# A fused attention and two-mixture kernel: rounding of h, one weight factor, router rounds and x sums issued at other products of the second mixture

## The chip, the cores and the metric

The kernel runs on one core of one Trainium2 chip. The metric is the device time of one execution in microseconds (us). Five engines work side by side, each through its own list of instructions in order: TensorE (PE, with PEld for its weight loads), VectorE (DVE), ScalarE (ACT), GpSimd (POOL) and SyncE (SP, which here only issues transfers). They wait for each other through semaphores.

## The reference

Three stages follow each other. Each step below computes only the third.

```python
# 1. clustered attention, 2 x 8 heads, 768 positions, 64 wide -> x (1536 tokens x 512)
# 2. first mixture: h = x @ w_in (512 x 2048); x = silu(h) @ w_out
# 3. second mixture: 8 experts, 1024 wide each
logits = x @ w_gate
P = np.exp(logits - logits.max())
for _ in range(8):                       # the router: 8 rounds
    P /= P.sum(1, keepdims=True) + 1e-09
    P /= P.sum(0, keepdims=True) + 1e-09
    P *= N / E
for e in range(E):
    h = np.maximum(x @ w1[e], 0.0)
    out += P[:, e:e + 1] * (h @ w2[e])
```

## The kernel before

**The stage in question.** The second mixture runs in 16 steps (`s` from 0 to 15), each half an expert: 512 of its 1024 hidden columns. A step is 14 turns of a loop over `n` (`s, i = divmod(n, 14)`, L1325). Turns 0 to 6 compute h = x @ w1, turns 7 to 13 compute h @ w2. Each of the two is a block product with 7 multiplications in place of 8 (Strassen's scheme), so most turns hold one *product*: 7 sums of blocks are multiplied and added into four results. One of the seven in the first layer is done once more in the same way on quarter blocks (`quad`, L1016: seven small products into the banks `q` and, in turn 7, `r`).

**Two parts for each factor.** TensorE multiplies fp32r. Each factor is split into a rounded part and a rest, and three matmuls (`hi*hi`, `hi*lo`, `lo*hi`) stand for one (L645). The rounded part of a weight factor is `wfh`, a copy by ScalarE (`factor_hi`, L848); the rest `wfl` is a subtraction by VectorE (`factor_lo`, L842). For h the parts are `ah` (`h_hi`, L1067, ScalarE) and `al` (`h_lo`, L1077, VectorE), each in two halves k = 0 and 1, of 768 tokens each. In the program's full names `ah3_9_1` is the rounded second half of the factor for scheme number 3 in step 9. There are four buffers for `ah` and four for `al`.

**Order.** The engines follow the order in which Python issues the instructions (`manual_schedule`, L1323): in each turn first the evacuation of the product before, then the preparation of factors for later products, then the matmuls of the turn's own product. Products of the second layer are multiplied half by half: 18 matmuls of 256 columns that use half 0 of h, then 18 that use half 1.

**Evacuation.** The second layer's scheme numbers come in the order 1, 5, 6, 3, 7, 2, 4 (turns 7 to 13). Numbers 1, 6, 7, 4 add up in one set of three PSUM banks and 5, 3 in another, and after each product the set is scaled by the router's column `Pg` and copied into a staging slot (`evacuate_b`, L1106; `acc` in the trace). So the set that a product adds into must have been evacuated during the product before it. In turns 11 and 12 VectorE copies the last bank, otherwise ScalarE copies all three (six instructions). A transfer of 768 KB then adds the slot to the output, issued by GpSimd (L1146). Slots are four slices of the buffer `acc1`, taken in turn (`stage`, L1101). In step 0 two of these slices still hold x.

**First layer.** `evacuate_a` (L1148) adds or copies the banks into h: by ScalarE (`copy_out`, `L1061`) or VectorE (`add_out`, the adds at L747). In turn 5 VectorE adds product 4 into the block `22`; ScalarE copies the same banks into the block `21` as soon as each add has read and written, then applies Relu to `22` in place (L1163). In turn 6 VectorE adds product 5 into `12`. Turn 6 has no product of its own in steps 1 to 15; turn 7 mixes the quarter products `r` with the first product of the second layer (L1041). `h_s1` to `h_s4` form the block sums of h on VectorE (L1165 to L1182).

**Router.** A generator `gate` (L940) holds the router; each `next(gating)` at the end of a turn issues it up to the next `yield`. A round is nine small VectorE instructions with one 8-column matmul `col` between them (L982 to L995).

**x sums.** `x4_sums` (L898) forms four sums of quarters of x in place in slice 3 of `acc1` on VectorE; `x4_rest(i)` (L903) splits one of them into its two parts (one ScalarE copy, one VectorE subtraction, 128x384). The quarter products `r` use them from step 1 on.

Of the kernel before, what the change touches and what calls it, by code (L numbers as in the profile page):

```python
# [38 lines left out]
def attention_moe_kernel(ctx, tc, kq, vp, cent, w_in, w_out, w_gate, w1, w2, out):  # L39
# [406 lines left out]
    with tc.manual_schedule(engines={ENG.PE, ENG.DVE, ENG.Activation, ENG.Pool, ENG.SP}):  # L446
# [147 lines left out]
        for pair in range(-4, NPAIR + 4):  # L594
            for item in ORDER:
                kind, at, *place = item.split(",")
                f, stride, low, high = KINDS[kind]
                i = int(at) + stride * pair
# [304 lines left out]
    def x4_rest(*which):  # L903
        hi, lo = (t[:, 3:] for t in x4)
        for i in which:
            act.copy(hi[:, i], x4_sum(i))
            lo_of(vec, lo[:, i], x4_sum(i), hi[:, i])
# [187 lines left out]
        return to[i * HT : (i + 1) * HT, j * HD : (j + 1) * HD].rearrange("(t p) d -> p t d", p=P)  # L1095

    stages, stores = [0], [0]
    RING = (0, 1, 2, 0, 1, 2, 0)
    kept = {}

    def stage():  # L1101
        stages[0] += 1
        n = stages[0] - 1
        return acc2[:, RING[n] if n < 7 else (3, 1, 2, 0)[(n - 7) % 4]]

    def evacuate_b(n, by_vec=0):  # L1106

# [86 lines left out]
    for s in range(NS1):  # L1194
        n = 2 * s + 1
# [122 lines left out]
    Pg = sk.tile([P, TT, E], F32, name="Pg")  # L1318

    gating = None  # L1320
    acc2 = acc1.rearrange("p k (t d) -> p k t d", d=HD)
    ENG = mybir.EngineType
    with tc.manual_schedule(engines={ENG.PE, ENG.DVE, ENG.Activation, ENG.Pool}):  # L1323
        psn = {}
        for n in range(14 * NS + 1):  # L1325
            s, i = divmod(n, 14)

            if i == 8:
                h_hi(s, 6, 1)
            if i == 2 or i == 7 and s:  # L1330
                pass
            elif n and i <= 7 and i > 0:
# [20 lines left out]
            if i == 1:  # L1353
                quad_add(s, 1)
                quad_add(s, 2)
                if s == 0:
                    x_factor(5, (0, 1))
                else:
                    quad_sums(s, True)
                if s == 1:  # L1360
                    x4_rest(0, 1)
            if i == 3:
                factor(n + 2, vec)
                factor(n + 3, vec)
# [7 lines left out]
                factor(n + 3, vec)  # L1372
                w_t3(n + 3, vec)
            if i == 4 + (s == 0):
                h_hi(s, 1, 0, relu=True)
                h_hi(s, 1, 1, relu=True)
                h_lo(s, 1, 0, relu=True)
                h_lo(s, 1, 1, relu=True)
            if i in (5, 6, 7) and 3 <= s < 7:
                for m in (2 * i - 10, 2 * i - 9):  # L1380
                    gps.tensor_scalar(out=again[:, m], in0=again[:, m], scalar1=Pg[:, 6 * block[0] + m, 0:1], scalar2=1.0, op0=ALU.mult, op1=ALU.mult)
                if i == 7:
                    gps.dma_start(out=out_block(*block), in_=again, accum_op=ALU.add)
            if i == 5 or i == 6 and s == 0:
                factor(n + 3, vec)
            if i == 5 and s == 0:
                x4_sums()
            if i == 6:
                h_s1(s, (0,))
                h_hi(s, 5, 0)  # L1390
# [10 lines left out]
                kept[1, 0] = stage()  # L1401
                nc.sync.dma_start(out=kept[1, 0], in_=out_block(1, 0))
            if i == 8:
                h_lo(s, 6, 1)
                h_s3(s)
            lates = {8: 3, 9: 7, 10: 2, 11: 4}
            late = lates.get(i - 1)
            if late:
                h_hi(s, late, 1, late == 2)
                h_lo(s, late, 1, late == 2)  # L1410
            if i == 9:
                h_s4(s)
            late = lates.get(i)
            if late:
                h_hi(s, late, 0, late == 2)
                h_lo(s, late, 0, late == 2)
            if i in (8, 9):
                factor(n + 2, vec)
            if i in (10, 11, 12, 13):
                if i == 11:  # L1420
                    w_t4(n - 4, vec)
                if i == 12:
                    w_load(n + 9)
                    w_sums1(n + 2, vec)
                factor(n + 2, vec)
                if i == 13:
                    quad_sums(s + 1)
            p = order(n)[i % 7]
            if i == 0:
                g = groups1(n, ready.pop(n), xf[1])  # L1430
                sets[n // 7, 1] = [ps3.tile([P, 512], F32, name=f"a{s}_1_{u}", tag="s") for u in range(3)]
                psn[n] = psn[n + 2] = sets[n // 7, 1]
                multiply(psn[n], g[:2], True)
                quad(s, 1)
                multiply(psn[n], g[2:], True)
                quad(s, 2)
            elif i == 1:
                g = groups1(n + 1, ready.pop(n + 1), xf[6])
                quad(s, 5)
                multiply(psn[n + 1], g[:1], False)  # L1440
                quad(s, 6)
                multiply(psn[n + 1], g[1:2], False)
                quad_add(s, 5)
                quad_add(s, 6)
                if s == 0:
                    x_sum((0, 0), t2, (0, 0), (0,))
            elif i == 2:
                quad(s, 7)
                multiply(psn[n], g[2:3], False)
                quad(s, 3)  # L1450
                multiply(psn[n], g[3:], False)
                quad_add(s, 7)
                if s == 0:
                    x_sum((0, 0), t2, (0, 0), (1,))
                quad(s, 4)
                quad_add(s, 3)
                if s == 0:
                    x_factor(7, (0, 0), (0,))
                quad_add(s, 4)
                ready.pop(n - 1)  # L1460
                factor(n + 2, vec)
                if s == 0:
                    x_factor(7, (0, 0), (1,))
                    x_factor(3, (1, 1))
                w_sums1(n + 5, vec)
                if s == 1:
                    x4_rest(2, 3)
            elif i == 6:
                if s == 0:
                    psn[n] = whole4(s, n)  # L1470
            elif i < 7:
                psn[n] = product(n, groups1(n, ready.pop(n), xf[p]))
            elif i == 7 and s:
                for q in (2, 1, 5):
                    quad(s, q, True)
                g = groups2([hf.pop((s, p, k)) for k in range(2)], ready.pop(n))
                psn[n] = sets[n // 7, 1] = [ps3.tile([P, 512], F32, name=f"b{s}_1_{u}", tag="s") for u in range(3)]
                opened = set()
                half_product(psn[n], g, 0, slice(0, 6), opened)
                quad_add(s, 2, True)  # L1480
                quad_add(s, 1, True)
                quad_add(s, 5, True)
                h_s1(s, (1,))
                h_hi(s, 5, 1)
                quad(s, 6, True)
                quad(s, 3, True)
                half_product(psn[n], g, 1, slice(0, 3), opened)
                quad_add(s, 6, True)
                h_lo(s, 5, 0)
                factor(n + 2, vec)  # L1490
                quad_add(s, 3, True)
                quad(s, 7, True)
                half_product(psn[n], g, 1, slice(3, 6), opened)
                quad_add(s, 7, True)
                h_lo(s, 5, 1)
                quad(s, 4, True)
                ready.pop(n - 1)
                h_s2(s, (0,))
                h_hi(s, 6, 0)
                quad_add(s, 4, True)  # L1500
                h_s2(s, (1,))
                h_lo(s, 6, 0)
            else:
                psn[n] = product(n, groups2([hf.pop((s, p, k)) for k in range(2)], ready.pop(n)), by_half=n < 14 * NS - 1)
# [3 lines left out]
            if gating is not None:  # L1508
                if s == 2 and i == 7:
                    for _ in gating:  # L1510
                        pass
                elif s == 0 or s < 3 and 2 <= i < 7 - s % 2 or s == 1 and i > 9:
                    next(gating, None)


# [36 lines left out]
```

## Time and profile before

| what | us |
| --- | --- |
| median of 3 runs | 1522.07 |
| lowest, highest | 1521.46, 1524.11 |
| the profiled execution's own time | 1523.46 |
| its span in the trace | 1521.7 |

The trace is of one execution. Its rows name an engine, a line, an operation and `out<-in` by the program's names without buffer numbers. Idle time that stands in brackets at a row is the time just before it in which its engine did nothing, and what ended it. A matmul's duration in the trace is longer than the distance to the next one, since matmuls overlap; how far TensorE is behind is read from the distances of their starts. The attention and the first mixture take the first 486 us, and the second mixture the rest.

### The profile page before, as it was taken

Reading aid. Unit: us, or ns where it says so; the run is one execution under the profiler, and the core shown is the slowest. Engines: PE = TensorE matmul, PEld = TensorE weight load, DVE = VectorE, ACT = ScalarE, POOL = GpSimd, SP = SyncE. Lnnn points to the kernel's source line nnn. Section 1 sums busy time; section 2 is a strip of 40 time slices with the busy share of each in tenths; the row PEclk is TensorE's granted clock in tenths of the full one; section 3 lists DMA queues with packets and bytes.
Section 4 is the critical chain, followed back from the end, with each engine's and each line's share of the span. In section 5 each row is a group of like instructions: output and inputs, shape, how many; then the busy total and the mean of one; then the engine's idle time right before and its main releaser. Section 6 shows DMA issues by size and latency. Waiting matters only on the chain.

```text
span 1521.7 us, 25357 instructions
## 1 busy us (share of the span) xinstructions
PE 1460.9 (96%) x9703; PEld 1298.5 (85%) x9704; DVE 1207.8 (79%) x2045; ACT 965.4 (63%) x1848; POOL 367.4 (24%) x356
## 2 busy tenths in 40 slices
PE   8999999999999999989999999999999999999997
PEld 5777778888888888889989889898898988999887
DVE  7788888678888878877887778778777777877777
ACT  7776777564563574656757667576675766757654
POOL 6776741212110010102212232021120211201111
PEclk9999999999999999999999999999999999999998
DMA  7667501212120072928769697494784947849566
GB/s 223 169 160 197 145 29 56 70 56 83 56 84 1 29 173 48 161 83 180 114 129 185 109 192 116 87 180 78 143 131 80 190 67 138 137 84 182 81 114 125
DMA packets 136314, 177.49 MB, mean 117 GB/s; under 512 B 6272, under 2 KB 108672, under 8 KB 136192
## 3 DMA queue, kind: packets, MB, share of 16 engines
q0 software_dynamic: 83584, 87.30, 38.0%
q1 hardware_dynamic: 51104, 87.32, 19.1%
q8 instruction: 76, 1.25, 0.3%
q10 hardware_dynamic: 1504, 1.25, 0.2%
q14 instruction: 46, 0.38, 0.1%
HBM read 65.36 MB, written 88.87 MB: 101 GB/s over the span
## 4 chain that ended last, share of the span: by engine, by line
PE 41%; DVE 19%; ACT 18%; issue 6%; ACTq 0%; DVEq 0%
PE b L652 12%; PE a L652 11%; PE y L706 9%; DVE h L747 6%; ACT acc L1137 6%; PE q L1021 4%; ACT ah L1074 3%; PE l L652 3%; ACT wfh L863 2%; DVE wfl L750 2%; DVE al L1082 2%; ACT h L1061 2%; DVE h L1168 2%; ACT h L1163 2%; DVE al L750 1%
## 5 line engine op out<-in xcount | busy, mean ns | idle before, releaser
L652 PE MATMUL b<-wfh,ah 128*128 128x256 f32 x1164 | 335.5, 288 | 14.1 <-ACT acc L1137 6.5
L652 PE MATMUL b<-wfh,al 128*128 128x256 f32 x1164 | 332.5, 286 | 4.6 <-DVE al L750 4.6
L652 PE MATMUL b<-wfl,ah 128*128 128x256 f32 x1164 | 331.7, 285 | 0.0
L1146 POOL DMA_DIRECT2D out_dram<-acc x87 | 126.2, 1580 | 618.6 <-ACT acc L1137 480.1
L1074 ACT CAST ah<-h 128x768 fp32r<-128x768 f32 x160 | 136.5, 853 | 181.0 <-DVE h L1168 83.1
L652 PEld LDWEIGHTS b<-wfh,ah 128*128 128x128 f32 x1164 | 223.4, 192 | 21.3 <-ACT acc L1137 9.4
L652 PEld LDWEIGHTS b<-wfh,al 128*128 128x128 f32 x1164 | 223.6, 192 | 8.2 <-DVE al L750 7.7
L652 PEld LDWEIGHTS b<-wfl,ah 128*128 128x128 f32 x1164 | 223.7, 192 | 2.2 <-DVE wfl L750 0.9
L652 PE MATMUL a<-xfh,wfh 128*128 128x512 f32 (+1 forms) x640 | 216.1, 338 | 0.4 <-ACT h L1061 0.2
L652 PE MATMUL a<-xfl,wfh 128*128 128x512 f32 (+1 forms) x640 | 215.8, 337 | 0.0
L652 PE MATMUL a<-xfh,wfl 128*128 128x512 f32 (+1 forms) x640 | 215.5, 337 | 0.0
L750 DVE TENSOR_TENSOR al<-h,ah 128x768 fp32r<-128x768 f32 x160 | 152.8, 955 | 77.8 <-ACT ah L1074 74.0
L1137 ACT ACTIVATE acc<-b,Pg 128x256 f32<-128x256 f32 x512 | 199.4, 507 | 0.0
L1061 ACT COPY h<-a 128x512 f32<-128x512 f32 x192 | 111.9, 605 | 136.2 <-PE a L652 92.2
L652 PEld LDWEIGHTS a<-xfh,wfh 128*128 128x128 f32 x640 | 121.1, 189 | 12.8 <-ACT h L1061 1.3
L652 PEld LDWEIGHTS a<-xfh,wfl 128*128 128x128 f32 x640 | 120.9, 189 | 12.9
L652 PEld LDWEIGHTS a<-xfl,wfh 128*128 128x128 f32 x640 | 121.1, 189 | 10.4
L313 ACT ACTIVATE p<-s,m 128x768 f32<-128x768 f32 x96 | 86.7, 905 | 39.4 <-DVE m L304 36.9
L304 DVE TENSOR_REDUCE m<-s 128x1 f32<-128x768 f32 x96 | 90.0, 951 | 13.5 <-PE s L297 13.1
L323 POOL TENSOR_SCALAR p<-p,rec 128x768 f32<-128x768 f32 x96 | 86.7, 915 | 48.6 <-DVE rec L318 41.4
L750 DVE TENSOR_TENSOR wfl<-w1r,wfh 128x512 fp32r<-128x512 f32 x80 | 55.0, 688 | 53.1 <-ACT wfh L863 53.1
L747 DVE TENSOR_TENSOR h<-q,h 128x384 f32<-128x384 f32 x112 | 60.8, 554 | 36.8 <-PE q L1021 34.8
(260 smaller groups left out, 3404.3 us busy)
## 6 DMA issues: line engine op xcount, KB each, us to landing
out_dram<-acc POOLq DMA_DIRECT2D x91, 768.0 KB, 9.3
w0r<-in_w_dram SPq DMA_DIRECT2D x16, 1024.0 KB, 5.1
w1r<-in_w_dram SPq DMA_DIRECT2D x16, 1024.0 KB, 6.6
qk<-qk SPq DMA_DIRECT2D x45, 192.0 KB, 3.5
wr<-in_w_in_dram SPq DMA_DIRECT2D x16, 512.0 KB, 3.7
wr<-in_w_out_dram SPq DMA_DIRECT2D x16, 512.0 KB, 3.5
first_out<-acc POOLq DMA_DIRECT2D x10, 768.0 KB, 10.5
raw<-in_kq_dram SPq DMA_DIRECT2D x16, 384.0 KB, 4.4
```

The costliest lines, as they stand in the source:

```text
L304: nc.vector.tensor_reduce(out=m, in_=tiles[i]["s"][:, :S], axis=AX.X, op=ALU.max, negate=True)
L313: nc.scalar.activation(t["p"], t.pop("s")[:, :S], AF.Exp, bias=t.pop("m"), accum_out=chunks[c]["sum"][:, j, 0:1])
L323: nc.gpsimd.tensor_scalar(out=p, in0=p, scalar1=chunks[c]["rec"][:, j : j + 1], scalar2=1.0, op0=ALU.mult, op1=ALU.mult)
L652: nc.tensor.matmul(ps[u][:, cols], lhsT=lf(i, k), rhs=rt(j, k), start=fresh and u not in opened, stop=k == 1 and q == 2, skip_group_check= ...
L706: nc.tensor.matmul(out, lhsT=w[:, k, d * P : (d + 1) * P], rhs=g, start=first, stop=last, skip_group_check=True)
L747: e.tensor_tensor(out=out, in0=in0, in1=in1, op=op)
L750: e.tensor_tensor(out=lo, in0=x, in1=r(hi), op=ALU.subtract)
L1021: nc.tensor.matmul(ps, lhsT=quad_lhs(s, q, a, four), rhs=(x4 if four else xq)[b][:, XQ[q]], start=j == 0 and q in (1, 2, 5), stop=j == 2, ...
L1061: act.copy(bank(t, u), ps[u])
L1074: act.copy(hi, x)
L1137: act.mul(t[:, 2 * u + m], z[:, m], g)
L1146: gps.dma_start(out=to, in_=t, accum_op=ALU.add)
```

## The change

It touches only the loop over `n` of the second mixture. No instruction's work changes; on TensorE only a few of the router's `col` matmuls stand elsewhere.

- **Second halves of h.** In turns 8 to 12 the second half of the factor for the next product (`h_hi(s, late, 1)`, and its `h_lo`) is issued at the head of the turn, ahead of the evacuation. Before, it came after the evacuation (for number 6, only its `h_lo` did).
- **One weight factor.** In turn 5 `factor_hi(n + 3)` (the rounded part of the weight factor for product 8) is issued ahead of `evacuate_a`, and its `factor_lo` after it. Before, both came after. In step 0 the Relu casts of number 1 move ahead of it too.
- **x sums.** `x4_sums` moves from turn 5 of step 0 to turn 11; `x4_rest(0)` and `(1)` from turn 1 of step 1 to turns 12 and 13 of step 0, `x4_rest(2)` and `(3)` from turn 2 of step 1 to places between the quarter adds of its turns 1 and 2.
- **Slots.** Since slice 2 holds x for longer, the ring of slots of the first two steps is written down anew: in step 0 slices 0 and 1 alternate, slice 2 comes fifth.
- **Router rounds.** Steps 1 and 2 draw `next(gating)` in turns 2, 3 (twice) and 4, where it was turns 2 to 5 (step 1) and 2 to 6 (step 2). Step 0 and turns 10 to 13 of step 1 draw as before.

```diff
-    RING = (0, 1, 2, 0, 1, 2, 0)
+    RING = (0, 1, 0, 1, 2, 0, 1)
...
-        return acc2[:, RING[n] if n < 7 else (3, 1, 2, 0)[(n - 7) % 4]]
+        return acc2[:, RING[n] if n < 7 else (3, 0, 2, 1)[(n - 7) % 4]]
...
+    LATES = {7: 6, 8: 3, 9: 7, 10: 2, 11: 4}
+    ROUNDS = {**{(0, i): 1 for i in range(14)}, (1, 2): 1, (1, 3): 2, (1, 4): 1, **{(1, i): 1 for i in range(10, 14)}, (2, 2): 1, (2, 3): 2, (2, 4): 2}
...
-            if i == 8:
-                h_hi(s, 6, 1)
+            late = LATES.get(i - 1)
+            if late:
+                h_hi(s, late, 1, late == 2)
+                h_lo(s, late, 1, late == 2)
+            if i == 5:
+                factor_hi(n + 3)
+                if s == 0:
+                    h_hi(s, 1, 0, relu=True)
+                    h_hi(s, 1, 1, relu=True)
             if i == 2 or i == 7 and s:
                 pass
             elif n and i <= 7 and i > 0:
                 evacuate_a(n - 1)
...
-                if s == 1:
-                    x4_rest(0, 1)
...
-            if i == 5 or i == 6 and s == 0:
+            if i == 5:
+                factor_lo(n + 3, vec)
+            if i == 6 and s == 0:
                 factor(n + 3, vec)
-            if i == 5 and s == 0:
-                x4_sums()
...
             if i == 8:
-                h_lo(s, 6, 1)
                 h_s3(s)
-            lates = {8: 3, 9: 7, 10: 2, 11: 4}
-            late = lates.get(i - 1)
-            if late:
-                h_hi(s, late, 1, late == 2)
-                h_lo(s, late, 1, late == 2)
...
+                if s == 0:
+                    if i == 11:
+                        x4_sums()
+                    if i > 11:
+                        x4_rest(i - 12)
...
+                if s == 1:
+                    x4_rest(2)
...
+                if s == 1:
+                    x4_rest(3)
...
-                if s == 1:
-                    x4_rest(2, 3)
...
-                elif s == 0 or s < 3 and 2 <= i < 7 - s % 2 or s == 1 and i > 9:
+                for _ in range(ROUNDS.get((s, i), 0)):
                     next(gating, None)
```

On ScalarE in turns 4 and 5 of step 9, before the change (`ah1` are the Relu casts for number 1, `h21` the block copies, `wfh134` the weight factor of product 8):

```order
L1072 ACTIVATE ah1_9_0_11785<-h11_9_11669 128x768
L1072 ACTIVATE ah1_9_1_11787<-h11_9_11669 128x768
L1061 COPY h21_9_11820<-a9_1_0_11633 128x512
L1061 COPY h21_9_11820<-a9_1_2_11635 128x512
L1061 COPY h21_9_11820<-a9_1_1_11634 128x512
L1163 ACTIVATE h22_9_11776<-h22_9_11776 128x768 x2
L863 CAST wfh134_11826<-w1r9_11512 128x512
L1074 CAST ah5_9_0_11858<-h12_9_11731 128x768
```

The same stretch with the change:

```order
L1072 ACTIVATE ah1_9_0_11785<-h11_9_11669 128x768
L1072 ACTIVATE ah1_9_1_11787<-h11_9_11669 128x768
L863 CAST wfh134_11817<-w1r9_11512 128x512
L1061 COPY h21_9_11823<-a9_1_0_11633 128x512
L1061 COPY h21_9_11823<-a9_1_2_11635 128x512
L1061 COPY h21_9_11823<-a9_1_1_11634 128x512
L1163 ACTIVATE h22_9_11776<-h22_9_11776 128x768 x2
L1074 CAST ah5_9_0_11858<-h12_9_11731 128x768
```

The factor's copy has moved ahead of the three block copies and the two Relus.

On ScalarE in turns 8 to 10 of step 9, before the change (`acc1<-b9_5` evacuates product 8, scheme number 5, and `acc1<-b9_1` product 9, number 6):

```order
L1074 CAST ah3_9_0_11960<-h12_9_11731 128x768
L863 CAST wfh136_11964<-w1r9_11512 128x512
L1137 ACTIVATE acc1_3475<-b9_5_0_11968,Pg_5397 128x256 x2
L1137 ACTIVATE acc1_3475<-b9_5_1_11969,Pg_5397 128x256 x2
L1137 ACTIVATE acc1_3475<-b9_5_2_11970,Pg_5397 128x256 x2
L1074 CAST ah3_9_1_12014<-h12_9_11731 128x768
L1074 CAST ah7_9_0_12020<-h11_9_11669 128x768
L863 CAST wfh137_12024<-w1r9_11512 128x512
L1137 ACTIVATE acc1_3475<-b9_1_0_11872,Pg_5397 128x256 x2
L1137 ACTIVATE acc1_3475<-b9_1_1_11873,Pg_5397 128x256 x2
L1137 ACTIVATE acc1_3475<-b9_1_2_11874,Pg_5397 128x256 x2
L1074 CAST ah7_9_1_12071<-h11_9_11669 128x768
```

With the change:

```order
L1074 CAST ah3_9_0_11960<-h12_9_11731 128x768
L863 CAST wfh136_11964<-w1r9_11512 128x512
L1074 CAST ah3_9_1_12007<-h12_9_11731 128x768
L1137 ACTIVATE acc1_3475<-b9_5_0_11968,Pg_5397 128x256 x2
L1137 ACTIVATE acc1_3475<-b9_5_1_11969,Pg_5397 128x256 x2
L1137 ACTIVATE acc1_3475<-b9_5_2_11970,Pg_5397 128x256 x2
L1074 CAST ah7_9_0_12020<-h11_9_11669 128x768
L863 CAST wfh137_12024<-w1r9_11512 128x512
L1074 CAST ah7_9_1_12064<-h11_9_11669 128x768
L1137 ACTIVATE acc1_3475<-b9_1_0_11872,Pg_5397 128x256 x2
L1137 ACTIVATE acc1_3475<-b9_1_1_11873,Pg_5397 128x256 x2
L1137 ACTIVATE acc1_3475<-b9_1_2_11874,Pg_5397 128x256 x2
```

`ah3_9_1` and `ah7_9_1` have each moved ahead of one evacuation; the evacuations themselves have kept their order.

On VectorE in turns 1 and 2 of step 1, before the change (`x4l` are the rests of x sums, `h11` the quarter adds, `qs1` sums of weights):

```order
L747 TENSOR_TENSOR qs1_6192<-w0r1_5560,qs1_6192 128x128 x2
L750 TENSOR_TENSOR x4l_5391<-acc1_3475,x4h_5390 128x384 x2
L747 TENSOR_TENSOR h11_1_6186<-q1_0_6165,h11_1_6186 128x384
L747 TENSOR_TENSOR h11_1_6186<-q1_2_6167,h11_1_6186 128x384 x2
L747 TENSOR_TENSOR h11_1_6186<-q1_0_6165,h11_1_6186 128x384
L747 TENSOR_TENSOR h11_1_6186<-q1_2_6167,h11_1_6186 128x384
L750 TENSOR_TENSOR wfl18_6246<-w0r1_5560,wfh18_6245 128x512
```

With the change:

```order
L747 TENSOR_TENSOR qs1_6196<-w0r1_5560,qs1_6196 128x128 x2
L747 TENSOR_TENSOR h11_1_6190<-q1_0_6169,h11_1_6190 128x384
L747 TENSOR_TENSOR h11_1_6190<-q1_2_6171,h11_1_6190 128x384
L750 TENSOR_TENSOR x4l_5391<-acc1_3475,x4h_5390 128x384
L747 TENSOR_TENSOR h11_1_6190<-q1_2_6171,h11_1_6190 128x384
L750 TENSOR_TENSOR x4l_5391<-acc1_3475,x4h_5390 128x384
L747 TENSOR_TENSOR h11_1_6190<-q1_0_6169,h11_1_6190 128x384
L747 TENSOR_TENSOR h11_1_6190<-q1_2_6171,h11_1_6190 128x384
L750 TENSOR_TENSOR wfl18_6250<-w0r1_5560,wfh18_6249 128x512
```

The pair of `x4l` ahead of the quarter adds is gone (it stands in step 0 now), and two others stand singly between later adds.

## Rows read from the trace of the kernel before

**Rows 1.** Page, busy time of each engine, its share of the span, instructions.
```profile
PE 1460.9 (96%) x9703; PEld 1298.5 (85%) x9704; DVE 1207.8 (79%) x2045; ACT 965.4 (63%) x1848; POOL 367.4 (24%) x356
```

**Rows 2.** Chain in order of time: start, us, engine, line, matmuls.
```profile
485.86 2.76 PE a L652 x12
...
693.85 2.75 PE a L652 x12
...
1447.80 2.75 PE a L652 x12
```

**Rows 3.** Timeline of PE, step 9: start, us, what, idle before.
```profile
1110.51 0.28 PE L652 MATMUL b<-wfh,ah 128*128 128x256 f32 x1
...
1119.03 0.28 PE L652 MATMUL b<-wfh,al 128*128 128x256 f32 x1
```

**Rows 4.** Timeline of PE, step 9, where it waits.
```profile
1097.77 0.38 PE L1041 MATMUL b<-wfh,ah 128*128 128x256 f32 x1 [0.19 <-DVE h L747]
...
1100.96 0.44 PE L1021 MATMUL r<-x4h,wqh 128*128 128x384 f32 x1 [0.78 <-DVE h L747]
...
1105.33 0.44 PE L1021 MATMUL r<-x4h,wfh 128*128 128x384 f32 x1 [0.39 <-DVE h L747]
...
1119.78 0.38 PE L652 MATMUL b<-wfh,ah 128*128 128x256 f32 x1 [0.47 <-ACT acc L1137]
1120.12 0.39 PE L652 MATMUL b<-wfl,ah 128*128 128x256 f32 x1
...
1122.95 0.39 PE L652 MATMUL b<-wfh,al 128*128 128x256 f32 x1 [0.30 <-DVE al L750]
1123.17 0.28 PE L652 MATMUL b<-wfh,ah 128*128 128x256 f32 x1
```

**Rows 5.** Timeline of ACT, step 9.
```profile
1092.62 1.79 ACT L1061 COPY h<-a 128x512 f32<-128x512 f32 x3 [2.34 <-DVE h L747]
...
1112.60 2.34 ACT L1137 ACTIVATE acc<-b,Pg 128x256 f32<-128x256 f32 x6
1114.75 0.91 ACT L1074 CAST ah<-h 128x768 fp32r<-128x768 f32 x1
1117.63 0.84 ACT L1074 CAST ah<-h 128x768 fp32r<-128x768 f32 x1 [1.97 <-DVE h L747]
...
1118.89 2.29 ACT L1137 ACTIVATE acc<-b,Pg 128x256 f32<-128x256 f32 x6
```

**Rows 6.** Timeline of DVE, step 9.
```profile
1091.90 1.88 DVE L747 TENSOR_TENSOR h<-a,h 128x512 f32<-128x512 f32 x3
1096.42 0.69 DVE L750 TENSOR_TENSOR wfl<-w1r,wfh 128x512 fp32r<-128x512 f32 x1 [2.64 <-ACT wfh L863]
1097.03 1.88 DVE L747 TENSOR_TENSOR h<-a,h 128x512 f32<-128x512 f32 x3
...
1115.69 0.96 DVE L750 TENSOR_TENSOR al<-h,ah 128x768 fp32r<-128x768 f32 x1 [1.88 <-ACT ah L1074]
1116.57 1.82 DVE L747 TENSOR_TENSOR h<-h,h 128x768 f32<-128x768 f32 x2
```

**Rows 7.** Timeline of PE, steps 0, 1 and 15, where it waits.
```profile
522.18 0.35 PE L652 MATMUL b<-wfh,ah 128*128 128x256 f32 x1 [2.86 <-DVE h L747]
...
566.57 0.44 PE L1021 MATMUL q<-xqh,wqh 128*128 128x384 f32 x1 [1.40 <-DVE h L747]
...
588.53 0.46 PE L1041 MATMUL b<-wfh,ah 128*128 128x256 f32 x1 [2.51 <-DVE h L747]
...
1510.80 0.58 PE L652 MATMUL b<-wfh,ah 128*128 128x256 f32 x1 [2.22 <-ACT ah L1074]
```

**Rows 8.** Windows of PE: us, busy, matmuls, granted clock, DMA, GB/s.
```profile
588.00:592.00 4.00, 3.47 (x17) 0.59 0.00 0
1510.80:1517.00 6.20, 6.00 (x26) 0.50 0.67 221
```

**Rows 9.** DMA issues: queue, count, KB each, median us to landing.
```profile
out_dram<-acc POOLq DMA_DIRECT2D x91, 768.0 KB, 9.3
```

## What the prediction said

> **What bounds the kernel now.** I read the page's busy times first. TensorE is busy for 96% of the span, VectorE for 79%, ScalarE for 63% [rows 1], so TensorE is the engine whose waits count; the question is how much it waits in the second mixture and for whom. The chain in order of time gives the length of the steps: the same piece of the first product begins steps 3 and 15 at 693.85 and 1447.80, so a plain step lasts 753.95 / 12 = 62.83 us, and steps 0 to 2 last (693.85 - 485.86) / 3 = 69.33 us on average [rows 2].
>
> Then TensorE's timeline of one plain step, step 9. In an undisturbed stretch 71 starts of 256 columns take 8.52 us, 0.12 us each [rows 3]. Five times a matmul waits [rows 4]: twice for VectorE's adds into h around turn 7 (0.19 and 0.78 us), once more at 1105.33 (0.39), at the start of product 11 for ScalarE's evacuation of product 9 (0.47), and within product 11 for VectorE's rest of h (0.30). A wait costs more than its idle time. At product 11 the next start was due at 1119.15 and came at 1119.78, 0.63 late for 0.47 idle; the one after came 0.34 later in place of 0.12, another 0.22. After the wait at 1122.95 the following start comes 0.22 later, 0.10 too late. I take 0.16 + 0.10 = 0.26 us on top of each idle time. The two stops of product 11 so cost 0.63 + 0.22 + 0.30 + 0.26 = 1.41 us, the three around turn 7 cost 1.36 + 3 x 0.26 = 2.14 us: 3.55 us of each step.
>
> Perfetto Trace Analysis in the Trainium skill, section Identifying the Most-Contended Engine, says that the matmul busy share is no good measure of headroom, since overlapped matmuls look different in a trace. The trace agrees: the idle times of a step add up to 2.13 us, the lost starts to 3.55. By the idle times alone 13 steps could give 28 us; I go by the starts.
>
> **Part 1: the weight factor ahead of the block copies.** In turn 5 ScalarE sits idle for 2.34 us until VectorE has added product 4 into its block; only after three copies and two Relus does it round the factor of product 8. VectorE, done with its adds at 1091.90 + 1.88 = 1093.78, waits 2.64 us for that factor, and its adds of product 5 stand behind it until 1097.03 [rows 5, 6]. With the change the rounding (one instruction of about 0.6 us, by the 0.69 of its VectorE partner at most) lies in ScalarE's idle 2.34 us. VectorE goes on at 1093.8, spends 0.6 on the rest (1096.42 to 1097.03), and reaches the adds of product 5 at about 1094.4. It cannot finish them before TensorE has finished product 5. TensorE is idle until 1097.77 for 0.19 after nine `r` matmuls that follow product 5; at 0.12 us at least each, product 5 was done by 1097.58 - 1.08 = 1096.5. The last add starts then at the latest, so the adds end by 1097.2 and not at 1098.91: VectorE is 1.7 us or more early from there. All three waits around turn 7 (0.19, 0.78, 0.39) are for VectorE's later adds in the same queue, and 1.7 covers the longest with its restart. Gain 2.14 us per step. Ends: all of it, or half if ScalarE's own casts of h hold VectorE up again.
>
> **Part 2: second halves first.** Before, ScalarE evacuates product 8 from 1112.60 to 1114.75 and then casts the second half of number 3. VectorE waits 1.88 us for that cast, starts the rest at 1115.69, then forms the block difference of h at 1116.57; ScalarE waits 1.97 us for the difference, casts number 7 at 1117.63, rounds a factor, and starts to evacuate product 9 at 1118.89, when TensorE wants the bank at 1119.15 [rows 4 to 6]. With the change the second-half cast starts at 1112.60 and takes 0.91 at most, so the evacuation of product 8 runs from 1113.5 to 1115.65. VectorE's rest starts at 1113.5, the difference 0.88 later at 1114.4 (its first half out at 1115.3). The cast of number 7 starts at 1115.65 with no wait; it and the factor behind it take 1.26 (1117.63 to 1118.89), number 7's second half 0.84, and the evacuation of product 9 starts at 1117.75, 1.1 us earlier than before although one more cast stands ahead of it. Its first bank is free after two of six instructions, 0.76 later at 1118.5, before 1119.15. The rest of number 7's second half is ready by about 1119, wanted at 1119.15 + 18 x 0.12 = 1121.3. Both stops go: 1.41 us.
>
> What waits behind the moved cast: the next evacuation always does, 0.84 us per product. In turn 12 it stands behind the last second half, and product 13 wants that set of banks; the trace shows no price, so between 0 (ScalarE is early) and 0.84 (the whole cast), and I take 0.15, nearer to 0, since in turns 11 and 12 ScalarE evacuates with four instructions in place of six. Its load for a full product here is 2.15 + 1.26 + 0.84 = 4.25 us against TensorE's 36 x 0.12 = 4.32, so it just keeps pace. Net per plain step 2.14 + 1.41 - 0.15 = 3.4 us; 13 steps (3 to 15): 44.2 us. Ends: 2.14 / 2 = 1.1 us, and 4.2 if small late starts that I did not price go too.
>
> **Part 3: steps 0 to 2 and the end.** Step 0 loses 2.86 + 0.26 us to VectorE's adds [rows 7]; four x sums (at most 0.63 each, a third of the 1.88 for three larger adds [rows 6]) now leave that queue. Moved to turn 11 they hold up the evacuation into slice 2, by 4 x 0.63 = 2.5 us at most. With the usual 3.4 I take 3.1 + 3.4 - 2.5 = 4.0, cut to 3 for the slots that return after two products rather than three in this step. Step 1: the usual 3.4; the wait of 2.51 in place of 0.19 goes for the same reason as in part 1 (2.3); the 1.40 + 0.26 goes as the pair of x parts leaves its place (1.7); and the granted clock is 0.59 in the 4 us after the long wait [rows 8], which is 1.6 us, and comes back if the wait goes. That is 9.0, less what the `col` matmul may wait now, since two router stretches are drawn in one turn with nine small VectorE instructions between; such a stretch also stood ahead of the wait at 588.53, so 2.3 us bounds it, and I take that whole: 6.7, rounded to 6.5. Step 2 has no such pair: 6. The router's other moves I cost at nothing: VectorE is idle for a fifth of the span [rows 1], and if it were not, a stretch would cost its 2.3 us in two steps. In step 15 TensorE waits 2.22 for the second-half cast of the last product, which stood behind ScalarE's transfers, and the clock is 0.50 for the next 6.2 us, 3.1 us lost. Of these 5.6 I take 5, since VectorE's final adds then follow close. Sum for part 3: 3 + 6.5 + 6 + 5 = 20.5.
>
> All together 44.2 + 20.5 = 64.7 us off the profiled execution's 1523.46: 1458.8. Its span is 1521.7, so 1.8 lie around it and stay. The median of the runs is 1.4 below that execution: 1457.4, and I say 1458.
>
> **Rivals.** (a) Only part 1 works: ScalarE keeps pace by less than 0.1 us per product, so any lateness of VectorE puts each evacuation where it was. Then 13 x 2.14 = 28, two thirds of part 3, 13: 1522 - 41 = 1481. For it: ScalarE's load. Against: the waits of 1.88 and 1.97 that part 2 takes out are on ScalarE's own path. (b) The stores set the pace. A slot comes back after four products, 4 x 4.32 - 2.15 = 15.1 us after its evacuation; a store lands after 9.3 us [rows 9]. If denser work lets it land at 18, one evacuation per step waits 2.9 us, 13 x 3.16 = 41 given back: 1498. Against: 5.8 us of margin. SBUF — State Buffer in the Trainium skill, section Who interferes with whom, speaks for it: VectorE operations with two SBUF inputs contend with GpSimd's reads, and transfers that GpSimd issues can starve. No row here shows such a delay. (c) Slower: each second-half cast needs the buffer of the same half two products earlier, which TensorE reads until that product's end. If it holds up the evacuation behind it past 3.6 us after a product's end (4.32 less the first bank's 0.72), five evacuations per step come 0.84 + 0.26 late each, 5.5 us, against 2.14 won: 16 x 3.4 = 54 us, 1576. Against: evacuations start well within that limit now, and the worked times put product 9's earlier. (d) The waits only change names: 1522.
>
> **How the numbers follow.** Forecast 0.80, (a) 0.11, (b) 0.05, (c) 0.03, (d) 0.01. The range reaches down to 4.2 us per step (13 x 0.8 less, with the clock: 1445) and up past (a) to 1486. A change of 0.2% is about what these runs can tell from none. Faster by more: forecast, (a), (b) = 0.96; same 0.01; slower 0.03.
>
> **What would show it.** Plain steps of 59 to 59.7 us; in a step no wait of TensorE above 0.3 us; VectorE's wait for the turn-5 factor gone and the next adds within 0.7 us of product 5's end; evacuation of product 9 starting before product 10 ends by more than a microsecond; no clock below 0.9 in steps 1 and 2. Wrong if TensorE waits for `acc` at product 11 or 13 by more than 0.5 us in each step, if a `col` matmul stops it for over 2.5 us, or if ScalarE waits for a landing.

## The result, and the profile after

The changed kernel takes 1453.88 us (median of four runs, 1453.45 to 1454.51), the kernel before 1522.66 in the same comparison. The ratio is 0.9548, its 95% interval 0.9532 to 0.9565. The forecast was 1458, with a range of 1445 to 1486.

The page of the changed kernel first: busy time of each engine, and the shares of the chain that ended last.

```profile
PE 1432.2 (99%) x9703; PEld 1290.1 (89%) x9704; DVE 1207.1 (83%) x2045; ACT 965.3 (66%) x1848; POOL 367.3 (25%) x356
...
PE 71%; DVE 7%; ACT 3%; issue 2%; DVEq 0%; ACTq 0%
```

No engine has less to do: VectorE and ScalarE are busy for the same microseconds as in [rows 1], and 70 us of span are gone. TensorE is busy for 28.7 us less with the same 9703 matmuls, because part of what a wait costs is counted as busy time. The chain in order of time (start, us, engine, line, matmuls) has the same first product of steps 0, 3 and 15 as [rows 2]:

```profile
486.69 2.76 PE a L652 x12
...
677.38 2.75 PE a L652 x12
...
1385.61 2.75 PE a L652 x12
```

A plain step lasts (1385.61 - 677.38) / 12 = 59.02 us, where it was 62.83. The waits of TensorE in the whole second mixture, 484 to 1452 us, are now these (total, times, longest):

```profile
PE r L1021 <- DVE h L747: 2.3, 4, 0.8
PE b L652 <- DVE acc L1116: 2.0, 2, 1.6
PE col L991 <- DVE cs L987: 0.9, 2, 0.4
PE b L652 <- ACT acc L1130: 0.8, 1, 0.8
PE q L1021 <- DVE h L747: 0.4, 1, 0.4
```

All of them lie in steps 0 to 2 and at the very end. In a plain step the view lists none (it leaves out idle times under 0.15 us), so nothing answers to [rows 4]. ScalarE in step 9 (timeline, as [rows 5]; turn 5 first, then turns 8 to 10):

```profile
1051.71 0.62 ACT L863 CAST wfh<-w1r 128x512 fp32r<-128x512 f32 x1 [1.49 <-issue]
1052.56 1.78 ACT L1061 COPY h<-a 128x512 f32<-128x512 f32 x3 [0.23 <-DVE h L747]
1054.24 1.58 ACT L1163 ACTIVATE h<-h 128x768 f32<-128x768 f32 x2
...
1069.26 0.86 ACT L1074 CAST ah<-h 128x768 fp32r<-128x768 f32 x1
1069.98 0.66 ACT L863 CAST wfh<-w1r 128x512 fp32r<-128x512 f32 x1
1070.50 0.87 ACT L1074 CAST ah<-h 128x768 fp32r<-128x768 f32 x1
1071.24 2.33 ACT L1137 ACTIVATE acc<-b,Pg 128x256 f32<-128x256 f32 x6
1073.57 0.84 ACT L1074 CAST ah<-h 128x768 fp32r<-128x768 f32 x1
1074.31 0.61 ACT L863 CAST wfh<-w1r 128x512 fp32r<-128x512 f32 x1
1074.83 0.83 ACT L1074 CAST ah<-h 128x768 fp32r<-128x768 f32 x1
1075.57 2.28 ACT L1137 ACTIVATE acc<-b,Pg 128x256 f32<-128x256 f32 x6
```

The factor now sits in the idle time of turn 5, and between the evacuations of products 8 (1071.24) and 9 (1075.57) ScalarE does not stop once: the wait of 1.97 us is gone. VectorE in the same step, as [rows 6]:

```profile
1051.85 1.88 DVE L747 TENSOR_TENSOR h<-a,h 128x512 f32<-128x512 f32 x3
1053.64 0.68 DVE L750 TENSOR_TENSOR wfl<-w1r,wfh 128x512 fp32r<-128x512 f32 x1
1054.24 1.28 DVE L747 TENSOR_TENSOR h<-a,h 128x512 f32<-128x512 f32 x2
1055.97 0.69 DVE L747 TENSOR_TENSOR h<-a,h 128x512 f32<-128x512 f32 x1 [0.45 <-PE a L652]
```

The wait of 2.64 us for the factor is gone; at 1055.97 it is VectorE that waits for TensorE. The stops of [rows 7] are gone. The longest that are left in steps 0, 1 and 15:

```profile
547.52 0.38 PE L652 MATMUL b<-wfh,ah 128*128 128x256 f32 x1 [0.75 <-ACT acc L1130]
...
582.96 0.44 PE L1021 MATMUL r<-x4h,wqh 128*128 128x384 f32 x1 [0.71 <-DVE h L747]
...
1442.41 0.36 PE L652 MATMUL b<-wfh,ah 128*128 128x256 f32 x1 [1.60 <-DVE acc L1116]
```

The last of them is not new. The kernel before has it too, at the same place, ahead of the stop of 2.22 us:

```profile
1507.99 0.35 PE L652 MATMUL b<-wfh,ah 128*128 128x256 f32 x1 [1.47 <-DVE acc L1116]
```

The granted clock in the stretches that answer to [rows 8] is full (the number before the last two), and a store still lands after the time of [rows 9]:

```profile
587.00:591.00 4.00, 3.66 (x27) 3.48 (x28) 4.00 (x6) 1.37 (x2) 0.00 (x0) 1.00 0.00 0
1442.40:1448.60 6.20, 4.54 (x36) 4.34 (x36) 6.13 (x16) 0.00 (x0) 0.00 (x0) 1.00 1.08 317
```

```profile
out_dram<-acc POOLq DMA_DIRECT2D x91, 768.0 KB, 9.3
```

### The profile page after: what moved, and what is told of

It reads as the page before. It is cut to its first block, busy times and chain, and to the rows that moved or that the text cites. A ratio compares the mean times of both kernels' runs of the same rounds, so it can differ in the third digit from the quotient of the medians.

```text
span 1452.1 us, 25386 instructions
## 1 busy us (share of the span) xinstructions
PE 1432.2 (99%) x9703; PEld 1290.1 (89%) x9704; DVE 1207.1 (83%) x2045; ACT 965.3 (66%) x1848; POOL 367.3 (25%) x356
## 4 chain that ended last, share of the span: by engine, by line
PE 71%; DVE 7%; ACT 3%; issue 2%; DVEq 0%; ACTq 0%
PE b L652 27%; PE a L652 20%; PE y L706 9%; PE q L1021 4%; PE b L1041 4%; PE r L1021 3%; PE l L652 3%; DVE h L747 1%; DVE wfl L750 1%; DVE acc L1116 1%; ACT h L674 1%; DVE h L678 1%; ACT acc L1137 0%; ACT gh L688 0%; ACT h L683 0%
## 5 line engine op out<-in xcount | busy, mean ns | idle before, releaser
L652 PE MATMUL b<-wfh,al 128*128 128x256 f32 x1164 | 329.1, 283 | 0.0
L652 PEld LDWEIGHTS a<-xfl,wfh 128*128 128x128 f32 x640 | 121.1, 189 | 10.3
L111 POOL TENSOR_TENSOR wr<-wr,u 128x512 f32<-128x512 f32 x32 | 44.2, 1383 | 183.2 <-DVE u L110 146.3
```

What stands on the lines that cost most here:

```text
L652: nc.tensor.matmul(ps[u][:, cols], lhsT=lf(i, k), rhs=rt(j, k), start=fresh and u not in opened, stop=k == 1 and q == 2, skip_group_check= ...
```

## The experiments

Length of the steps in us, from the start of each step's first matmul (a plain step is the mean of steps 3 to 14; the last column runs to the end of the span):

| kernel | step 0 | step 1 | step 2 | plain step | step 15 and end |
| --- | --- | --- | --- | --- | --- |
| before | 69.2 | 69.2 | 69.6 | 62.8 | 74.0 |
| part 1 alone | 66.7 | 66.4 | 65.8 | 60.8 | 71.8 |
| part 2 alone | 68.2 | 67.7 | 65.4 | 61.1 | 68.7 |
| part 3 alone | 70.8 | 66.5 | 68.6 | 62.9 | 73.0 |
| parts 1 and 2 | 65.7 | 64.1 | 62.7 | 59.1 | 66.8 |
| changed | 65.4 | 62.6 | 62.6 | 59.0 | 66.7 |

**Part 1 alone.**

```diff
+            if i == 5:
+                factor_hi(n + 3)
...
-            if i == 5 or i == 6 and s == 0:
+            if i == 5:
+                factor_lo(n + 3, vec)
```

> The kernel before with part 1 alone (the weight factor of product 8 ahead of the block copies in turn 5). Theory S (the stops around turn 7 and those of product 11 are separate losses): the three waits around turn 7 go, 2.1 us in each of 15 steps, and 3.9 more in step 1 (the 2.51 us wait and the lower clock after it), 36 us: about 1486 us; the waits of 0.47 for the evacuation and 0.30 for the rest of h at product 11 stay, plain steps 60.7 us. Rival Q (one cause: VectorE comes late out of turn 5 and carries its lateness to product 11): part 1 alone takes nearly all of the 3.8 us of a plain step, 59.0 us each, the whole about 1465. Rival E (ScalarE's order decides): plain steps above 61.5 us, the whole above 1500.

Measured: 1487.86 us, ratio 0.9762 (0.9749 to 0.9776). TensorE's waits in step 9 are the two of product 11 and no others:

```profile
1097.09 0.38 PE L652 MATMUL b<-wfh,ah 128*128 128x256 f32 x1 [0.63 <-ACT acc L1137]
1100.26 0.38 PE L652 MATMUL b<-wfh,al 128*128 128x256 f32 x1 [0.30 <-DVE al L750]
```

Theory S holds, plain steps of 60.75 us where 60.7 were expected. Q falls: VectorE comes out of turn 7 on time, and product 11 waits all the same. In step 0 the edit also puts the Relu casts of number 1 earlier. VectorE no longer waits for them, as it did in the kernel before:

```profile
516.72 1.83 DVE L1082 SCALAR_TENSOR_TENSOR al<-h,ah 128x768 fp32r<-128x768 f32 x2 [2.38 <-ACT ah L1072]
```

TensorE's wait at product 7 falls with it from 2.86 to 0.39 us.

**Part 2 alone.**

```diff
+            late = LATES.get(i - 1)
+            if late:
+                h_hi(s, late, 1, late == 2)
+                h_lo(s, late, 1, late == 2)
...
-            lates = {8: 3, 9: 7, 10: 2, 11: 4}
```

> The kernel before with part 2 alone (second halves of h rounded ahead of the evacuation in turns 8 to 12). Theory S: both waits of product 11 go, 1.4 us less 0.15 in each of 16 steps, and 5 us at the last product with its lower clock, 25 us: about 1497 us; the waits of 0.19, 0.78 and 0.39 around turn 7 stay, plain steps 61.5 us. Rival Q: VectorE is still late, product 11 waits as before, only the end gains: plain steps 62.6 us, about 1516. Rival E: plain steps 59.5 or less, about 1470.

Measured: 1491.17 us, ratio 0.9786 (0.9773 to 0.9799), six below S. The three waits around turn 7 stand as in [rows 4], and product 11 has none:

```profile
1081.05 0.39 PE L1041 MATMUL b<-wfh,ah 128*128 128x256 f32 x1 [0.19 <-DVE h L747]
1084.24 0.44 PE L1021 MATMUL r<-x4h,wqh 128*128 128x384 f32 x1 [0.77 <-DVE h L747]
1088.62 0.44 PE L1021 MATMUL r<-x4h,wfh 128*128 128x384 f32 x1 [0.40 <-DVE h L747]
```

S holds in its places; its size was 1.26 us per step and measured 1.75.

**Part 3 alone.** The edit is all that the diff ahead changes in slots, x sums and router rounds.

> The kernel before with part 3 alone (x sums, slots and router rounds). Theory S: plain steps stay at 62.8 us; step 0 gains at most 3 us, step 1 the 1.66 us of the wait at its quarter products, step 2 little since its pair of stretches now stands nearer to turn 7: about 1518 us, between 1514 and 1522. Rival: the moved sums hold up the evacuations of step 0 and the pairs of router stretches stop TensorE 2.3 us each, 1525.

Measured: 1520.84 us, ratio 0.9984 (0.9975 to 0.9993), hardly more than these runs can tell. In step 0 one wait has taken the place of another. Product 7's is down from 2.86 to 0.74 us, and product 13 now stands for the evacuation of product 11 into slice 2, for which ScalarE waits 2.47 us until VectorE has formed the x sums:

```profile
550.39 0.39 PE L652 MATMUL b<-wfh,ah 128*128 128x256 f32 x1 [2.88 <-ACT acc L1130]
```

The granted clock from 551 to 554 us is 0.50.

**Parts 1 and 2.** Both edits above together.

> The kernel before with parts 1 and 2, without part 3. Theory S: the gains of the two runs with one part each add up to within 3 us, plain steps 59.0 us, the whole about 1461, 7 us above the changed kernel. Rival (the parts overlap, each removes the other's waits too): the sum of the two single gains is over 8 us more than the gain of both. Rival (the parts need each other): it is over 8 us less.

Measured: 1456.74 us, ratio 0.9559 (0.9546 to 0.9572), against 0.9548 (0.9532 to 0.9565) for the changed kernel: the intervals overlap. Against the 1523.72 us of the kernel before in these runs, the single gains are 35.9 and 32.6 us, 68.4 by their sum before rounding; both parts at once give 67.0. They add up. By the table, part 3 is worth 1.5 us in step 1 and little elsewhere.

**Which second half.** Part 1, and of part 2 the second half of number 3 only.

```diff
+            if i == 9:
+                h_hi(s, 3, 1)
+                h_lo(s, 3, 1)
...
-            if late:
+            if late and late != 3:
```

> The kernel before with part 1, and of part 2 only the second half of number 3 (turn 9) ahead of the evacuation; the other four second halves stay behind theirs. Theory O (one cast holds the chain up: it delays VectorE's rest and its block difference, the cast of number 7 and so the evacuation of product 9): both stops of product 11 go, plain steps 59.0 to 59.3 us, and only the end of step 15 keeps its wait of 2.2 us with the low clock, 4 us: about 1461 us. Rival M (the order counts at each product: what moves for number 3 alone makes another evacuation or second half late): plain steps 59.8 us or more, about 1470.

Measured: 1458.06 us, ratio 0.9574 (0.9559 to 0.9588). Theory O holds: plain steps last 58.84 us, 0.2 less than with all five moved. One cast stood at the head of the chain that [rows 5, 6] show. The other four moves earn nothing in a plain step. Steps 1 and 2 last 1.5 and 1.1 us longer here than with parts 1 and 2 whole; which move earns that was not tested. The move of number 4 earns in step 15, where this kernel still has the old stop, with a clock of 0.72 in the six microseconds from 1446:

```profile
1446.31 0.47 PE L652 MATMUL b<-wfh,ah 128*128 128x256 f32 x1 [2.22 <-ACT ah L1074]
```

The 0.2 us are the start of product 13. With all five moved it comes 0.07 + 0.11 us late, with this one it comes on time.

**Casts twice.** The changed kernel, with a second cast in `h_hi`.

```diff
+        if k and p in (3, 7, 2):
+            if relu:
+                act.activation(hi, x, AF.Relu)
+            else:
+                act.copy(hi, x)
```

> The changed kernel, where the casts of the second halves of numbers 3, 7 and 2 are issued twice on ScalarE, 0.75 us more for each; the second writes the same values. Theory L (evacuations may start up to 3.6 us after a product's end and start 2.4 us after it now, so 1.1 us are spare): the first extra cast costs nothing, the second leaves the bank of product 11 free 0.4 us late, the third that of product 12 0.3 us, with their restarts 1.0 to 1.3 us per step: 1470 to 1476 us, with waits of TensorE for acc at products 11 and 12. Rival (ScalarE has room, it is busy for 66% of the span): under 1457. Rival (ScalarE is the bound of this stretch already): the whole 2.25 us per step, 1490.

Measured: 1493.30 us, ratio 0.9803 (0.9788 to 0.9818): 61.57 us per plain step, 2.55 more. The third theory comes out, and L falls. ScalarE's evacuations of products 8 to 10 in step 9, and TensorE at products 11 to 13:

```profile
1092.36 0.83 ACT L1079 CAST ah<-h 128x768 fp32r<-128x768 f32 x1
1093.10 2.29 ACT L1142 ACTIVATE acc<-b,Pg 128x256 f32<-128x256 f32 x6
...
1098.15 2.29 ACT L1142 ACTIVATE acc<-b,Pg 128x256 f32<-128x256 f32 x6
...
1103.21 1.55 ACT L1142 ACTIVATE acc<-b,Pg 128x256 f32<-128x256 f32 x4
```

```profile
1099.03 0.38 PE L652 MATMUL b<-wfh,ah 128*128 128x256 f32 x1 [0.45 <-ACT acc L1142]
...
1104.09 0.39 PE L652 MATMUL b<-wfh,ah 128*128 128x256 f32 x1 [0.45 <-ACT acc L1142]
...
1109.26 0.38 PE L652 MATMUL b<-wfh,ah 128*128 128x256 f32 x1 [0.59 <-ACT acc L1142]
```

The evacuations start 5.05 us apart, and TensorE's products follow at 5.04, 5.06 and 5.17. ScalarE sets the pace as soon as its work per product (4.3 + 0.75) is above TensorE's 4.32. In the changed kernel product 10 starts at 1085.78 - 0.07 - 3 x 4.32 = 1072.75, and its first bank is free at 1071.24 + 2 x 0.36 = 1071.96; 0.16 us pass between the two where TensorE waits (1093.83 and 1093.99 here). So 0.6 us were spare, not the 1.1 that I had from product ends placed 0.4 us too late. That is used up once and never comes back: 3 x 0.75 - 0.6 = 1.65, and four restarts of 0.26 each make 2.7, against 2.55 measured.

**ScalarE evacuates all banks.**

```diff
-                evacuate_b(n - 1, by_vec=2 if i in (11, 12) else 0)
+                evacuate_b(n - 1, by_vec=0)
```

> The changed kernel, where ScalarE copies all three banks in turns 11 and 12 too (four instructions of 0.36 us more per step on ScalarE, four less on VectorE). Theory L: ScalarE waits 1.6 us in turn 12 anyway for VectorE's sum of weights, which takes up the two of turn 11; the two of turn 12 end 0.7 us before their bank is wanted: no change, 1454 us within 3, plain steps 59.0 us. Rival (ScalarE only just keeps pace, as the forecast said): 1.44 us per step in 13 steps with restarts, 1473 or more.

Measured: 1466.34 us, ratio 0.9627 (0.9612 to 0.9641), plain steps of 60.01 us. L falls again. ScalarE's wait in turn 12 is as long as before, and product 13 now waits:

```profile
1091.84 0.62 ACT L863 CAST wfh<-ws 128x512 fp32r<-128x512 f32 x1 [1.63 <-DVE ws L747]
```

```profile
1093.98 0.38 PE L652 MATMUL b<-wfh,ah 128*128 128x256 f32 x1 [0.67 <-ACT acc L1137]
```

The 1.63 us are no room. By the order of the program ScalarE casts number 4, VectorE forms its rest and then the sum of weights, and only then can ScalarE round that sum: when the cast comes 0.7 us later, all of it does.

**The sum of weights earlier, and the same with ScalarE evacuating.** To test that reading, the sum moves from turn 11 to turn 10, ahead of the cast.

```diff
+            if i == 10:
+                w_t4(n - 3, vec)
...
-                if i == 11:
-                    w_t4(n - 4, vec)
```

> The changed kernel, where VectorE forms the sum of weights of product 13 in turn 10, not in turn 11. Theory W (ScalarE's wait of 1.63 us in turn 12 is no room but the way there and back: rest of h, sum on VectorE, then the factor on ScalarE; the evacuation of product 11 hangs on it, and product 13 starts 0.18 us late for that): the wait goes, product 13 starts on time, plain steps 58.8 us, 1451.5 us. Rival (the 0.18 us come from elsewhere): 59.0 us, 1454.

> As the kernel with the earlier sum, and ScalarE copies all three banks in turns 11 and 12 (cost 0.98 us per step without the earlier sum). Theory W: now there is room for the two instructions of turn 11, which is where the cost was: plain steps 58.8 to 59.0 us, 1452 to 1455 us. Rival (ScalarE has no room in the stretch, however the sum stands): plain steps 59.7 us or more, 1463 or more.

> The changed kernel once more, to compare the next three with it in the same runs: 1454 us, plain steps 59.0 us.

Measured in one comparison: the changed kernel 1454.17 us, ratio 0.9550 (0.9537 to 0.9563); the earlier sum 1463.48, 0.9609 (0.9595 to 0.9622); the earlier sum with ScalarE evacuating 1459.27, 0.9583 (0.9570 to 0.9596). W holds as far as it goes: ScalarE no longer waits for `ws`, no plain step has a wait at product 13, step 3 lasts 58.8 us, and the four extra instructions on ScalarE cost nothing. But steps 4 to 14 last 59.0 to 61.0 us, and neither theory said why. ScalarE waits for a transfer in front of the evacuation of product 13:

```profile
1097.59 2.30 ACT L1137 ACTIVATE acc<-b,Pg 128x256 f32<-128x256 f32 x6 [4.09 <-DMA out_dram<-acc]
```

GpSimd's stores and SyncE's load of weights in step 9, first with the earlier sum, then in the changed kernel:

```profile
1083.84 1.44 POOL L1146 DMA_DIRECT2D out_dram<-acc  x1 [2.92 <-ACT acc L1137]
1098.11 5.87 POOL L1146 DMA_DIRECT2D out_dram<-acc  x4 [12.84 <-ACT acc L1137]
...
1085.75 0.37 SPq L757 DMA_DIRECT2D w1r<-in_w_dram  x1
```

```profile
1078.29 1.44 POOL L1146 DMA_DIRECT2D out_dram<-acc  x1 [2.92 <-ACT acc L1137]
1087.73 5.94 POOL L1146 DMA_DIRECT2D out_dram<-acc  x4 [8.00 <-ACT acc L1137]
...
1083.68 0.37 SPq L757 DMA_DIRECT2D w1r<-in_w_dram  x1
```

The sum was the last to read `w1r`. Read earlier, the buffer comes free earlier, and the 1 MB load begins 1.9 us after the store of product 9, where it was 5.4. From that store to the next issue now pass 12.5 to 14.3 us in steps 3 to 14, where it was 9.1 to 11.1 in two executions of the changed kernel. The slot is due back for product 13, and is late: that store lands at 1097.49, and ScalarE goes on at 1097.59. That the load's start delays the store was not tested alone: a kernel that holds the load back was not run.

**Router rounds earlier in step 2, alone and with the earlier sum.**

```diff
-    (2, 2): 1, (2, 3): 2, (2, 4): 2}
+    (2, 0): 1, (2, 1): 2, (2, 2): 2}
```

In step 2 the changed kernel draws twice in turn 4 as well as in turn 3.

> The changed kernel with the router's last draws in step 2 moved from turns 2 to 4 to turns 0 to 2, where VectorE waits for the quarter products. Theory V (the waits of 0.4 and 0.8 us at the quarter products r of turn 7 come from VectorE's router stretches just ahead): step 2 loses its waits for col and r, 2.4 us less, 60.3 us. Rival (the stretches then delay VectorE's quarter adds, and TensorE waits for h at the products q): step 2 as long as now, 62.6 us, or longer. The whole 1451.5 or 1454 us.

> The changed kernel with the earlier sum and the router's last draws in turns 0 to 2 of step 2 (that moved step 2 from 62.65 to 61.93 us). If both gains add up: 13 x 0.18 + 0.7 = 3 us less, 1451 us, just above what five rounds can tell. Rival: the moved draws or the sum make something else late, 1453 to 1456.

Measured: 1452.94 us, ratio 0.9537 (0.9521 to 0.9553), which these runs can't tell from the changed kernel. Step 2 is 0.7 us shorter: the waits for `col` and `r` are gone, and 1.24 + 0.28 us at the quarter products `q` have come, so each theory is half right. With the earlier sum too it is 1459.89, 0.9593 (0.9580 to 0.9606), held up by the same stores. None of these versions beats the changed kernel by more than these runs can tell. The move of number 3 alone in steps 3 to 14 would save 12 x 0.18 = 2.2 us by its plain steps; that is an estimate and less than these runs can tell, and it was not run with the rest of the change.

## Why the prediction was right, point by point

**The bound.** TensorE's lost starts were the right measure. A plain step lost 3.55 us by the starts, and 3.81 came back; the idle times alone had 2.13. The signs that the forecast named came: plain steps of 59.02 us with no listed wait, the evacuation of product 9 starting 1.5 us before product 10 ends (1075.57, product 11 starts at 1077.07), and a full clock in steps 1 and 2.

**Part 1**: 2.14 forecast, 62.83 - 60.75 = 2.08 measured alone. The mechanism is shown by its own rows: the factor in ScalarE's idle time, the three waits gone, the two of product 11 still there (0.63 and 0.30 us in step 9).

**Part 2**: 1.41 less 0.15 forecast, 1.75 measured alone. Starts that are late by a tenth, such as 0.13 + 0.10 at a quarter product, went as well; the forecast left them to the upper end of its range. The 0.15 at product 13 is there: 0.18. The mechanism is narrower than the forecast told it: of five moves one carries the plain step. And "it just keeps pace" is shown by the casts issued twice, which cost 2.55 us per step. The 0.99 us of the other experiment on ScalarE are not its load but the round trip behind VectorE's sum: with the earlier sum the same four instructions cost nothing.

**Part 3**, by what each place measured against the forecast:

- Step 0: 3 forecast, 3.8 measured, for another reason. The x sums were to free VectorE, and alone they do (2.86 to 0.74 us). But part 1 alone takes that wait down to 0.39, since its edit also puts the Relu casts of step 0 earlier, and moving the sums alone costs step 0 1.6 us. The bound of 2.5 us on the evacuation was about right: ScalarE waits 2.47 us for the sums with part 3 alone and 1.68 in the changed kernel, and TensorE 2.88 and 0.75 behind it.
- Step 1: 6.5 forecast and 6.5 measured, of which 5.1 come without part 3. That the two agree is luck in part. The `col` matmul was charged 2.3 us and waits 0.43; in its place 0.71 and 0.40 us remain at the products `r`, which the forecast took as gone.
- Step 2: 6 forecast, 7.0 measured, none of it from part 3. Its stop of 2.51 us at 655.96, with a clock of 0.59 in the next six microseconds, was the twin of step 1's. The forecast names neither, and gives no terms for its 6.
- The end: 5 forecast beyond the usual 3.4, 3.5 measured beyond the usual 3.8. The wait for the cast and the low clock are gone: the last matmul starts 61.22 us after the step's first, where it was 70.19. TensorE so gains 9.0 us, which is what 3.4 and 5.6 make. But from that last start to the end of the span now pass 5.46 us, where it was 3.84. VectorE's last add ends 1.86 us after it (1.20 before), and the last store lands 2.7 us after its issue (1.7 before). The forecast took 0.6 off for what follows TensorE; it was 1.6.

The sum came to 64.7 and the span lost 69.5: 12 x 0.41 = 5 us from the plain steps. The rest cancels by luck: steps 0 and 2 gave 1.8 us more than forecast, the whole of step 15 1.1 less, and the second mixture began 0.8 us later.

**The rivals.** (a) fell: part 2 gives its gain with or without part 1. (b) did not happen here, but its margin of 5.8 us was wrong. The evacuation of product 9 ends at 1077.85, its slot is wanted at 1089.50, and its store, issued at 1078.29, lands after 8.8 us at 1087.11: 2.4 us. The forecast had counted four whole products, but products 12 and 13 are evacuated close behind one another. The earlier sum of weights shows the rival at work, by a store that lands late where a load begins close behind it. SBUF — State Buffer in the Trainium skill (section Who interferes with whom) speaks for (b) less than the forecast had it: it says that VectorE's `tensor_tensor` with both inputs in SBUF contends with GpSimd's reads, but also that a probe saw no DMA stall from it. The changed kernel shows no such delay either: VectorE's share of the span rose from 79% to 83%, and a store landed after 9.3 us as before. (c) did not happen: in a plain step no moved cast makes TensorE late by more than the 0.18 us at product 13. What it would take to make evacuations late is more work on ScalarE: the casts issued twice cost 2.55 us per step.

## What to carry to other kernels

Price a wait by the starts that the bound engine loses, and look for the one instruction at the head of a chain between two other engines: here one cast moved ahead of one evacuation gave all that part 2 gives in a plain step. An engine busy for 66% of the span can have next to no room in the stretch that counts, and an idle time that is a round trip between two engines is not room either. A faster step moves the transfers too: before moving the last reader of a buffer, look at which store the freed buffer's load will then meet.

## What the runs showed of the hardware that was not expected

A store and a load took longer where they started closer together. In step 9 of the changed kernel the 768 KB store of product 9 landed 8.8 us after its issue, and the 1 MB load that began 5.4 us behind it took 7.3 us. With the earlier sum the load began 1.9 us behind, and they took 13.7 and 11.4 us. Over all steps the median of that load is 7.2 and 10.3 us. The store of product 10 adds to the same block of the output as that of product 9, and in both kernels it is issued 0.6 us after that one's landing. That the distance of the starts is the cause is argued, not shown, since nothing varied it alone.

The same wait does not always cost the clock. With part 2 alone TensorE waits 2.52 us for the same adds in steps 1 and 2, at 586.86 and at 652.53 us. The windows behind the two waits have a granted clock of 0.50, the level of 1.2 GHz, and of 1.00:

```profile
586.80:592.00 5.20, 5.14 (x22) 5.14 (x23) 4.42 (x8) 1.47 (x2) 0.00 (x0) 0.50 0.00 0
652.50:658.00 5.50, 3.84 (x27) 3.64 (x28) 5.29 (x12) 0.95 (x2) 0.00 (x0) 1.00 0.00 0
```

In the kernel before, the same wait of step 2 brought 0.59. What TensorE did ahead of the two waits differs: in step 1 it had waited 1.18 us some four microseconds earlier, in step 2 the view lists no wait in the ten microseconds ahead. But in the kernel before step 2 has none there either, and the clock fell; the cause stays open.
